# Two products exchanged in their shared bank, weight sums over two attentions, Strassen's form from block 2 on

## The chip, the core and the metric

The kernel runs on one core of a Trainium2 chip. The core has five engines with a queue of instructions each: TensorE (PE; its weight loads are listed as PEld), VectorE (DVE), ScalarE (ACT), GpSimd (POOL) and SyncE (SP), which here mostly issues DMAs. Matmuls write to PSUM, which has 8 banks; one bank holds 128 x 512 values of fp32. The metric is the time of one execution on the device in microseconds (us), as a median over runs.

## The reference

An attention with a relative position bias for 8 batches, 8 heads, 576 positions and head dimension 64, followed by a feed-forward layer with the activation h + sin(alpha h)^2 / alpha:

```python
scores = (q @ k.T) / 8 + bias_table[bucket(|i - j|)]
attn   = exp(scores - max); attn /= attn.sum(-1) + 1e-9
x      = (attn @ v) as [4608 tokens, 512]
h      = x @ w_in                      # 512 -> 2048
g      = h + sin(alpha * h)**2 / (alpha + 1e-9)
out    = g @ w_out                     # 2048 -> 512
```

Inputs and output are fp32 in memory; the kernel multiplies in fp16 and accumulates in fp32.

## The kernel before

There are 8 attentions t = 0 to 7 and 9 blocks of 512 tokens b = 0 to 8. After attention t comes the first half of the feed-forward layer for block t (`plan_moe_in`: for 16 slices f of 128 hidden channels four matmuls into one bank, a sine on ACT, a square on ACT or DVE, and one DVE instruction that writes slice f of the tile g). The second half of block t, g @ w_out, is cut into single matmuls that PE takes as filling work while the attention of t + 1 runs. Block 8 comes after block 7 at the end.

The order of all instructions is worked out when the program is built. `Plan.add` takes a step with its cost on each engine that may do it, what it depends on, a priority and the buffers it needs; `Plan.run` walks through time with these costs, always picks the step that can start first and among those that start together the one with the lowest priority number, and emits it to the queue of the engine that ends it first. So a changed cost can move a step to another engine or change the order of a queue. What waits for what at run time is then set by the dependences of the emitted instructions; between PE and a reader of PSUM they go by bank.

In an attention the scores of a head pair and 128 keys are two matmuls (`qT,kT`; `qT,kt` for the last 64 keys) into a pair of banks among (0,1), (2,3), (4,5); ACT takes the exponential (line 719) into u, or into the tile called nat for the last 64 queries; DVE multiplies a band of it by the exponential of the bias (lines 750, 736, 763, 728); nine matmuls per 128 queries (`vh,u` and eight `v,u`) form the product with v in bank 6 or 7; DVE divides by the row sum (lines 964, 965); and the result reaches xT by a DMA transpose or by PE (line 1036) with a copy on ACT or DVE. Before the first exponential and before the first sine ACT loads a table (line 1403).

The filling work has two forms. A plain row (`plan_mo`) is 128 tokens: 16 matmuls of 512 columns into one bank of tag "mo" (7 or 6), one copy of 128x512 to SBUF by DVE (line 551) and a store. A chain (`plan_chain`) does two such rows by Strassen's form in Winograd's variant: 7 products instead of 8, each of 8 matmuls of 256 columns, where 2k and 2k + 1 share one bank, halves 0 and 1. Products 0 to 5 use banks of tag "mo", product 6 one of tag "st" (any bank). The chain needs four sums of parts of g, each in four pieces of 128x256 on DVE (line 1311), and four sums of quarters of w_out (`wsum`), which are made once in the attention of block 1 (`plan_wsum`, line 1180). DVE reads each product and adds it to what it goes into (`take`, line 1367; the copy of product 0 into the tile zz is on line 551). Blocks 1 to 6 are done as two plain rows and one chain, in the order of MIX = "nnssss"; block 0 as four plain rows; blocks 7 and 8 in another Strassen form (`plan_half`) that the diff leaves alone.

The chain also carries, behind its last product, the step with which POOL copies k and q of attention b + 2 to the staging buffers (`stage_kq`); it depends on the loads of v (`plan_moe_in`) and on the chain's fourth sum. In attention 0 and 1 k and q are turned by PE (`plan_tr`) and copied out of PSUM by DVE or ACT (lines 551 and 549). `plan_late` puts the score units of the last 64 queries of attention 0 at the start of attention 1.

Of the kernel before, what the change touches and what calls it, by code (L numbers as in the profile page):

```python
# [58 lines left out]
class Cell:  # L59
    v = None  # L60
# [178 lines left out]
T_LD = 33.0  # L239

MIX = "nnssss"
CH = ("mo", "mo", "mo", "st")
PIECES = 4
AV_LATE = 9000
# [32 lines left out]
def kernel(  # L277
# [122 lines left out]
    def stage_kq(t):  # L400
        for dst, src in ((staged_k, k), (staged_q, q)):
            nc.gpsimd.dma_start(
                out=dst.ap()[t].rearrange("s (h d) -> s h d", h=H),
                in_=src[t].rearrange("h s d -> s h d"),
            )
# [135 lines left out]
    plan = Plan()  # L541
# [11 lines left out]
    def plan_tr(t, p, kq, pri, nb, deps=()):  # L553

        b, c = Buf("mo"), Cell()

        def mm(e):
            c.v = bank(b).bitcast(F16)
            for i in range(SI):
                x = i * SN  # L560
                if t == 0 and p == 0:
                    nc.tensor.transpose(  # L562
                        out=c.v[:, x : x + SN], in_=natb[:, kq, i], identity=id_sb[0:SN, 0:SN]
                    )
                    continue
                for z in range(2):
                    h = 2 * p - 2 + z if t == 0 else 2 * p + z
                    nc.tensor.transpose(  # L568
                        out=c.v[64 * z : 64 * z + 64, x : x + SN],
                        in_=(nat1 if t == 0 else nat2)[:, kq, h, D * i : D * i + D],  # L570
                        identity=id_sb[0:SN, 0:SN],
                    )

        def cp(e):
            pin = c.v[:, 0:S].rearrange("d (i p) -> d p i", i=SI)

            dst = (kTs, qTs)[kq][t][:, p, :]
            copy_on(e, dst.rearrange("d (p i) -> d p i", i=SI), pin)

        m = plan.add({"PE": 0.4 if t == 0 and p == 0 else 0.5}, mm, deps, pri, nb, new=[b])  # L580
        if t == 0:
            m.pad = (256,) if p else (192,) * (2, 3)[kq]
        eng = {"DVE": 0.75, "ACT": 0.6}
        if t == 0:
            eng = {"ACT": 0.65} if p in T_ACT and kq else {"DVE": 0.75}
        x = plan.add(eng, cp, [m], pri, use=[b])
        if kq:
            return [x], [x]

        def tail(e):  # L590
            for z in range(2):
                r = slice(64 * z, 64 * z + 64)
                k_of(e).tensor_copy(
                    out=kts[t][r, p, r], in_=kTs[t][r, p, 512:S]
                )

        return [x], [plan.add({"POOL": 0.4 if t == 0 else 0.5}, tail, [x], pri + 30)]
# [282 lines left out]
    def plan_late(base, gate):  # L880

        tb, done = tails[0] = Buf("ut"), {}
        units = [(0, "B", 0), (2, "B", 0), (0, "X", 0)]
        made = [plan_unit(0, *x, None, tb, done, gate, base + 30 * k) for k, x in enumerate(units)]

        def run(e):
            for x in made:
                x[2](e)

        m = plan.add({"PE": 0.78}, run, pe_gate, base, new=[tb] + [x[0] for x in made])  # L890
        m.offs = [0.0, 0.1, 0.32, 0.6]
        m.marks = [(x[1], o) for x, o in zip(made, (0.32, 0.54, 0.78))]
        tail_alone(0, base + 1200)
        return [x[3] for x in made]
# [235 lines left out]
    mo_last, kq_in, staged, to_stage = [], [], [], []  # L1130
# [33 lines left out]
    def plan_wsum(t, deps):  # L1164

        n = DM // 2
        quad = [[w_out16[:, NF // 2 * i : NF // 2 * i + NF // 2, n * j : n * j + n] for j in range(2)]
                for i in range(2)]
        todo = (
            (0, quad[0][1], quad[0][0]),  # L1170
            (1, quad[1][1], wsum[:, 0]),
            (2, quad[1][1], quad[0][1]),
            (3, quad[1][0], wsum[:, 1]),
        )
        k, x, y = todo[t]
        for i, d in enumerate(deps):
            r = slice(2 * i, 2 * i + 2)

            def sm(e, k=k, x=x, y=y, r=r):
                nc.vector.tensor_tensor(out=wsum[:, k, r], in0=x[:, r], in1=y[:, r], op=ALU.subtract)  # L1180

            wdone.append(plan.add({"DVE": 0.36}, sm, [d] + wdone[-4:], PB + 9500))

    wdone = []

# [102 lines left out]
    def plan_chain(b, a):  # L1288
# [8 lines left out]
        base = 500000000 + 4 * b + a  # L1297

        def act(i, j):
            return gcell[b].v[:, H2 * j : H2 * j + H2, 128 * (a + i) : 128 * (a + i) + 128]  # L1300
# [17 lines left out]
        def sums(k):  # L1318
            return sv.v[:, 2 * k : 2 * k + 2].rearrange("p k (f t) -> p (k f) t", f=H2 // 2)
# [9 lines left out]
        def prod(k, x, w, deps):  # L1329

            for f in range(H2):

                new = f == 0 and k % 2 == 0

                def mm(e, f=f, new=new):
                    if new:
                        bv[k // 2].v = bank(bk[k // 2])
                    full(at(k), x()[:, f], w()[:, f], f == 0, f == H2 - 1)

                mo_last[:] = [plan.add({"PE": t_pe(n)}, mm, mo_last[:] + deps, base,  # L1340
                                       new=[bk[k // 2]] if new else [],
                                       use=([] if new else [bk[k // 2]]) + [sb, gbuf[b]])]
                mo_last[0].fill = True
                mo_last[0].part = n / DM
            return mo_last[0]
# [4 lines left out]
        def ws(k):  # L1350
            return lambda: wsum[:, k]
# [24 lines left out]
        s2 = pre(lambda: sums(1), lambda: sums(0), lambda: act(0, 0), ALU.subtract, [s1])  # L1376
# [4 lines left out]
        p = prod(1, lambda: act(0, 1), wq(1, 0), [])  # L1381
        c11 = take(1, (0, 0), (2, 0), [p, x], True)
        yield
        p = prod(2, lambda: sums(1), ws(1), [s2, x] + wdone)
        y = take(2, (1, 1), (2, 0), [p, x], True)
        p = prod(3, lambda: act(1, 0), ws(2), [s3])
        v = take(3, (1, 0), (1, 1), [p, y])
        yield
        p = prod(4, lambda: sums(0), ws(0), [])
        w = take(4, (0, 1), (1, 1), [p, y])  # L1390
        c22 = take(4, (1, 1), (1, 0), [p, v, w])
        p = prod(5, lambda: act(1, 1), ws(3), [])
        take(5, (1, 0), (1, 0), [p, v, c22], last=True)
        yield
        p = prod(6, lambda: sums(2), wq(1, 1), [s4])
        take(6, (0, 1), (0, 1), [p, w, c11], last=True)
# [9 lines left out]
    PB = 0  # L1406
# [6 lines left out]
    for t in range(T):  # L1413
        PB = 1000000 * t

        if t > 0:
            gate = [plan.add({"ACT": D_TBL}, lambda e: set_table(EXP_SET), sins, PB)]
        exps = []
        for p in range(NP - 1) if t == 0 else ():
            for kq in range(2):  # L1420
                tr[(0, p + 1, kq)] = plan_tr(0, p + 1, kq, (150, 650, 5)[p], T_PAIR[p][kq])
        if t == 0:
            for g in range(2):
                exps += plan_att0(g, pe_gate, gate)
        else:
            exps += plan_att(t, pe_gate, gate)
            if t == 1:
                for i in range(4):
                    plan_wsum(i, exps[3 * i + 1 : 3 * i + 4] + exps[3 * i + 3 : 3 * i + 4])
            if t == 1:  # L1430
                exps += plan_late(PB + LATE, gate)
        if t == 0:
            for p in range(NP):
                for kq in range(2):
                    tr[(1, p, kq)] = plan_tr(1, p, kq, 10085 + 20 * p, T_TR1[kq])
            plan.add({"POOL": 5.0}, lambda e: stage_kq(2), [], 10090,
                     after=lds + [tr[(1, p, 0)][1][0] for p in range(NP)])

        def swap(e, t=t):
            set_table(SIN_SET)  # L1440
        def turn_in(e, t=t):
            load_kqT(t + 1)
            load_kt(t + 1)

        tbl = [plan.add({"ACT": D_TBL}, swap, exps, PB)]
        if 1 <= t < T - 1:
            kq_in.append(plan.add({"SP": 5.5}, turn_in, [], PB + 9000, after=tbl + [
                x for tt, _, _, x in xdone if tt == t and "SP" in x.engs]))
        if t == T - 1:
            tail_alone(t, PB + 10015)  # L1450
        sins = []
        for b in [t] if t < T - 1 else [t, t + 1]:
            m, s_ = plan_moe_in(b, tbl)
            sins += s_
        pe_gate = [m]
        if t < T - 1:
            if t:
                rows, ch = iter((0, 1)), plan_chain(t, 2)
                for x in MIX:
                    if x == "n":  # L1460
                        plan_mo(t, next(rows))
                    else:
                        next(ch)
            else:
                for a in range(4):
                    plan_mo(t, a)
        else:
            for b in (t, t + 1):
                for a in (0, 2):
                    plan_half(b, a)  # L1470
# [31 lines left out]
```

## Time and profile before

| what | value |
|---|---|
| median of three runs | 369.23 us (368.93 to 372.27) |
| profiled execution | 368.74 us |
| its span in the profile | 366.8 us |
| DMA | 40.53 MB, mean 110 GB/s |
| exponentials, line 719, 128x1024 | 1.03 us each |
| g, line 1094 | 0.74 us each, 144 of them |
| read of a product, line 1367 | 0.42 us each, 30 + 12 of them |

The table's durations are means of groups of instructions in the profiled execution. A record's length isn't the time that an instruction keeps its engine from the next one: neighbours overlap, on PE most of all. Where an engine's throughput matters, starts are compared with starts. The profile also follows the work that ended last backwards from the end (the chain of waits), and lists for each engine in order of time what ran and what ended an idle time before it.

### The profile page before, as it was taken

To read this page: it belongs to the slowest core of one execution; us is meant where nothing else is said; L and a number is where in the kernel's file an instruction comes from. 1 tells how busy PE (TensorE), PEld (TensorE's weight loads), DVE (VectorE), ACT (ScalarE), POOL (GpSimd) and SP (SyncE) were. 2 spreads that over 40 slices of the span, in tenths; PEclk is the share of its full clock that TensorE was granted. 3 is DMA by queue.
4 is the path that set the end of the run, shared out by engine and by line. 5 is a ranking of instruction groups with operands and counts; after the bars stand their busy time and mean duration, and the time that the engine had idled before them with its cause. 6 is when DMAs were issued, how large, how long until landed. Compare 5 with 4: busy or idle time off the path is not lost.

```text
span 366.8 us, 9604 instructions
## 1 busy us (share of the span) xinstructions
PE 356.8 (97%) x3808; PEld 218.9 (60%) x3808; DVE 309.2 (84%) x748; ACT 312.3 (85%) x430; POOL 92.0 (25%) x133
## 2 busy tenths in 40 slices
PE   7889999999999999999999999999999999999996
PEld 3464545644475446885684457545776468456685
DVE  4797979878977998699978998798869997899982
ACT  3988999889897999799988999799979997996711
POOL 7477350064000830047000900082006000000000
PEclk9999999999999999999999999999999999999999
DMA  9999999599724996299917992599529421001122
GB/s 170 198 172 204 200 162 148 115 97 122 111 53 102 127 150 108 78 143 113 152 52 153 87 173 55 134 125 128 104 79 163 35 79 50 15 2 57 44 74 87
DMA packets 150269, 40.53 MB, mean 110 GB/s; under 512 B 137208, under 2 KB 145616, under 8 KB 150224
## 3 DMA queue, kind: packets, MB, share of 16 engines
q0 software_dynamic: 96032, 17.67, 59.6%
q1 hardware_dynamic: 54016, 22.16, 25.9%
q8 instruction: 30, 0.49, 0.6%
q14 instruction: 15, 0.12, 0.1%
q10 hardware_dynamic: 176, 0.09, 0.1%
HBM read 37.73 MB, written 16.56 MB: 148 GB/s over the span
## 4 chain that ended last, share of the span: by engine, by line
PE 83%; ACT 10%; DVE 4%; issue 2%; ACTq 0%
PE pb L469 82%; ACT u L719 8%; ACT s L1080 1%; DVE outs L1367 1%; DVE u L750 1%; ACT sq L1087 1%; PE pb L1036 1%; PE pb L568 0%; ACT kT L549 0%; DVE nat L763 0%; ACT qT L549 0%; DVE xn L965 0%; PE pb L562 0%; DVE qT L551 0%; DVE zz L551 0%
## 5 line engine op out<-in xcount | busy, mean ns | idle before, releaser
L719 ACT ACTIVATE u<-pb 128x1024 f16<-128x1024 f32 (+1 forms) x146 | 136.8, 1022 | 10.3 <-PE pb L469 9.6
L469 PE MATMUL pb<-xT,w_in 128*128 128x512 f16 (+4 forms) x704 | 128.1, 340 | 0.0
L1094 DVE SCALAR_TENSOR_TENSOR g<-sq,inv_a,pb 128x512 f16<-128x512 f16 x144 | 101.1, 743 | 3.7 <-ACT sq L1087 2.0
L1080 ACT ACTIVATE s<-pb,alphaT 128x512 f16<-128x512 f32 x144 | 92.8, 693 | 12.8 <-PE pb L469 12.0
L469 PEld LDWEIGHTS <-w_in 128*128 128x128 f16 x704 | 64.7, 98 | 56.1 <-issue 0.3
L469 PE MATMUL pb<-w_out,g 128*128 128x512 f16 (+1 forms) x416 | 81.7, 339 | 0.5 <-DVE zz L551 0.5
L469 PEld LDWEIGHTS <-g 128*128 128x128 f16 x552 | 51.4, 98 | 37.6 <-issue 7.2
L750 DVE TENSOR_TENSOR u<-u,m2r 128x512 f16<-128x512 f16 (+1 forms) x128 | 61.6, 489 | 11.4 <-ACT u L719 8.6
L469 PEld LDWEIGHTS <-u 128*128 128x128 f16 x1280 | 56.0, 97 | 9.1 <-issue 3.8
L414 POOL COPY kt<-kT 64x256 f16<-64x256 f16 x12 | 5.2, 432 | 172.4 <-DMA kT<-staged_k 142.9
L1087 ACT ACTIVATE sq<-s 128x512 f16<-128x512 f16 x69 | 43.4, 639 | 2.0 <-DVE g L1094 1.1
L469 PE MATMUL pb<-qT,kT 64*128 64x64 f16 (+1 forms) x512 | 42.7, 285 | 1.8 <-DVE qT L551 0.6
L469 PE MATMUL pb<-v,u 128*128 128x65 f16 x1024 | 44.1, 193 | 0.3 <-DVE u L750 0.2
L1089 DVE TENSOR_TENSOR sq<-s 128x512 f16<-128x512 f16 x75 | 31.7, 432 | 10.8 <-ACT s L1080 10.1
L965 DVE TENSOR_TENSOR xn<-pb,rd 128x256 f16<-128x256 f32 (+2 forms) x59 | 28.5, 483 | 2.0
L469 PEld LDWEIGHTS <-kT 64*128 64x128 f16 x512 | 16.1, 94 | 22.4 <-issue 15.4
L469 PE MATMUL pb<-vh,u 128*128 128x130 f16 x128 | 28.2, 221 | 0.1
L419 POOL DMA_DIRECT2D v<-in_v_dram x28 | 24.8, 896 | 3.9 <-DMA nat<-in_k_dram 2.3
L1403 ACT ACT_TABLE_LOAD x15 | 19.2, 1283 | 0.3
L469 PE MATMUL pb<-wsum,g 128*128 128x256 f16 (+1 forms) x136 | 18.6, 266 | 0.9
L719 ACT ACTIVATE nat<-pb 128x1024 f16<-128x1024 f32 (+1 forms) x24 | 17.7, 817 | 0.0
L1367 DVE TENSOR_TENSOR outs<-pb,outs 128x256 f32<-128x256 f32 x30 | 12.6, 421 | 5.3 <-PE pb L469 4.7
(97 smaller groups left out, 303.0 us busy)
## 6 DMA issues: line engine op xcount, KB each, us to landing
out_dram<-outs SPq DMA_DIRECT2D x28, 256.0 KB, 2.9
v<-in_v_dram POOLq DMA_DIRECT2D x28, 128.0 KB, 4.5
staged_k<-in_k_dram POOLq DMA_DIRECT2D x6, 576.0 KB, 8.6
staged_q<-in_q_dram POOLq DMA_DIRECT2D x6, 576.0 KB, 12.4
w_in<-in_moe_w_in_dram POOLq DMA_DIRECT2D x4, 512.0 KB, 8.4
w_out<-in_moe_w_out_dram POOLq DMA_DIRECT2D x4, 512.0 KB, 14.7
out_dram<-outs SPq DMA_DIRECT2D x15, 128.0 KB, 1.7
w_out<-in_v_dram SPq DMA_DIRECT2D x6, 128.0 KB, 4.3
```

The lines of the kernel that those rows point to most:

```text
L414: nc.gpsimd.tensor_copy(out=kts[t % 2][r, :, r], in_=kTs[t % 2][r, :, 512:S])
L419: nc.gpsimd.dma_start(out=vs[t % 2][:, c, :, 0:D], in_=vp[128 * c : 128 * c + 128],)
L469: nc.tensor.matmul(out=out, lhsT=lhsT, rhs=rhs, start=start, stop=stop, skip_group_check=go_on)
L719: nc.scalar.activation(out=o, in_=x, func=AF.Exp, scale=0.125)
L750: nc.vector.tensor_tensor(out=io, in0=io, in1=m2[:, 2 * p : 2 * p + 2, x0 : x0 + hi - lo], op=ALU.mult)
L965: nc.vector.tensor_tensor(out=xn[:, 0:n].rearrange("p c (z d) -> p c z d", z=2), in0=x[:, :, :, 0:D], in1=r.unsqueeze(3).to_broadcast([128 ...
L1080: nc.scalar.activation(out=s16.v, in_=h.v, func=AF.Sin, scale=alphaT[:, f : f + 1])
L1087: nc.scalar.activation(out=sq.v, in_=s16.v, func=AF.Square)
L1089: k_of(e).tensor_tensor(out=sq.v, in0=s16.v, in1=s16.v, op=ALU.mult)
L1094: nc.vector.scalar_tensor_tensor(out=gcell[b].v[:, f, :], in0=sq.v, scalar=inv_a[:, f : f + 1], in1=h.v, op0=ALU.mult, op1=ALU.add,)
L1367: nc.vector.tensor_tensor(out=put(i, j), in0=at(k), in1=put(*x), op=ALU.add)
L1403: nc.scalar.preload_act_table_set(name)
```

## The change

In the chain, the order of products 4 and 5 in their bank is exchanged: the product of act(1,1) with the fourth weight sum is now number 4, that of the first sum of g with the first weight sum number 5. The result of the new product 4 is read last, after the two reads of product 5. Product 2 waited for the weight sums, for a sum of g and for the copy of product 0; the last of these is dropped.

Block 1 is done as four plain rows (FIRST = 2), and its staging step becomes a step of its own without the chain's sum ahead of it. The weight sums are made two in attention 1 and two in attention 2, each in eight pieces of 128x256 instead of four of 128x512, each piece after one exponential of the attention (every second from the third on). Two costs for the planner are lower: an ACT copy in `plan_tr` for attention 1, 0.6 to 0.53, and the late units of attention 0 on PE, 0.78 to 0.5.

```diff
+SUMS = {1: (0, 1), 2: (2, 3)}
+FIRST = 2
...
-        eng = {"DVE": 0.75, "ACT": 0.6}
+        eng = {"DVE": 0.75, "ACT": 0.53}
...
-        m = plan.add({"PE": 0.78}, run, pe_gate, base, new=[tb] + [x[0] for x in made])
+        m = plan.add({"PE": 0.5}, run, pe_gate, base, new=[tb] + [x[0] for x in made])
...
-            r = slice(2 * i, 2 * i + 2)
+            r = slice(i, i + 1)
...
-            wdone.append(plan.add({"DVE": 0.36}, sm, [d] + wdone[-4:], PB + 9500))
+            wdone.append(plan.add({"DVE": 0.218}, sm, [d] + wdone[-8:], PB + 9500))
...
-        p = prod(2, lambda: sums(1), ws(1), [s2, x] + wdone)
+        p = prod(2, lambda: sums(1), ws(1), [s2] + wdone)
...
-        p = prod(4, lambda: sums(0), ws(0), [])
-        w = take(4, (0, 1), (1, 1), [p, y])
-        c22 = take(4, (1, 1), (1, 0), [p, v, w])
-        p = prod(5, lambda: act(1, 1), ws(3), [])
-        take(5, (1, 0), (1, 0), [p, v, c22], last=True)
+        prod(4, lambda: act(1, 1), ws(3), [])
+        p = prod(5, lambda: sums(0), ws(0), [])
+        w = take(5, (0, 1), (1, 1), [p, y])
+        c22 = take(5, (1, 1), (1, 0), [p, v, w])
+        take(4, (1, 0), (1, 0), [p, v, c22], last=True)
...
-            if t == 1:
-                for i in range(4):
-                    plan_wsum(i, exps[3 * i + 1 : 3 * i + 4] + exps[3 * i + 3 : 3 * i + 4])
+            for i in SUMS.get(t, ()):
+                plan_wsum(i, exps[2:18:2])
...
-            if t:
+            if t >= FIRST:
...
             else:
                 for a in range(4):
                     plan_mo(t, a)
+                if to_stage:
+                    n_, x = to_stage.pop()
+                    plan.add({"POOL": 4.5}, lambda e, n_=n_: stage_kq(n_), [x], PB + 9600)
```

## The prediction

> **What bounds the kernel now.** I read the page first, then the chain of waits in order of time, then the timeline of TensorE (PE) beside VectorE (DVE) and ScalarE (ACT) at the places that the diff touches. The page:
>
> ```profile
> span 366.8 us, 9604 instructions
> PE 356.8 (97%) x3808; PEld 218.9 (60%) x3808; DVE 309.2 (84%) x748; ACT 312.3 (85%) x430; POOL 92.0 (25%) x133
> PEclk9999999999999999999999999999999999999999
> PE 83%; ACT 10%; DVE 4%; issue 2%; ACTq 0%
> ```
>
> PE is busy 97% of the span at the full granted clock, and 83% of the chain is PE. Busy alone proves little, because a matmul's record is longer than its turn. So I look at starts: a run of 64 matmuls and a run of 8 half-wide ones.
>
> ```profile
> 112.95 13.98 PE L469 MATMUL pb<-xT,w_in 128*128 128x512 f16 x64
> 145.10 1.04 PE L469 MATMUL pb<-wsum,ss 128*128 128x256 f16 x8
> 100.30 0.27 PE L469 MATMUL pb<-w_out,g 128*128 128x256 f16 x1 [0.51 <-DVE zz L551]
> 309.51 53.78 PE pb L469 x416
> ```
>
> Taking one record (0.38 us for a 512-wide matmul, half of the 0.76 us that two would take end to end; 0.27 us for a 256-wide one, third row) off each run, a 512-wide matmul takes a turn of (13.98 - 0.38) / 63 = 0.216 us and a 256-wide one (1.04 - 0.27) / 7 = 0.11 us, 0.109 over longer runs. Nearly everything on PE goes at those turns, and the last 54 us of the chain are one unbroken PE row. So the kernel is bound by PE's queue: time changes by the turns added or taken, and by the few waits inside that queue. The 2 us of waits on PE that this change can reach are what it is about.
>
> **The wait inside an attention.** First the chain for the attention of block 3, then the timeline of the same place.
>
> ```profile
> 143.88 5.19 PE pb L469 x92
> 149.09 0.42 DVE outs L1367
> 149.52 0.20 DVE nat L763
> 149.72 0.35 DVE outs L1367
> 150.10 1.58 PE pb L469 x13
> ```
>
> ```profile
> 148.78 0.27 PE L469 MATMUL pb<-wsum,g 128*128 128x256 f16 x1
> 148.95 0.41 PE L469 MATMUL pb<-v,u 128*128 128x65 f16 x8
> 149.09 0.42 DVE L1367 TENSOR_TENSOR outs<-pb,outs 128x256 f32<-128x256 f32 x1 [0.39 <-PE pb L469]
> 149.25 0.41 PE L469 MATMUL pb<-v,u 128*128 128x65 f16 x8
> 149.55 0.41 PE L469 MATMUL pb<-v,u 128*128 128x65 f16 x8
> 149.63 0.42 DVE L1367 TENSOR_TENSOR outs<-pb,outs 128x256 f32<-128x256 f32 x1
> 150.10 0.93 PE L469 MATMUL pb<-wsum,g 128*128 128x256 f16 x7
> ```
>
> Product 5 starts (one matmul at 148.78), then attention matmuls run, then its other seven stand until DVE has read product 4 twice out of the same bank, at 149.63 + 0.42 = 150.05. The chain puts 0.42 + 0.20 + 0.35 = 0.97 us of DVE there, but PE was working through the first part of it: one group of v,u begins 0.30 after the other (149.25, 149.55), of which the vh,u matmul between them (130 columns, at the same rate) has 0.06. So the last group's turns ended at 149.55 + 0.24 = 149.79, and PE went on at 150.10. It lost 0.31 us, not 0.97. That distinction carries the forecast.
>
> **The change part by part.**
>
> *Products 4 and 5 exchanged.* The product that is needed only at the end now goes first and is read only after the other is done; both are in the bank before DVE reads anything. In the built program the remaining matmuls of the second product carry no wait on DVE. Five attentions (3 to 7) keep such a chain: 5 x 0.31 = 1.55 us less. The three reads then come back to back after the pair, 2 x 0.35 = 0.7 us later for DVE than before. What hides that is DVE's own idle time behind this place:
>
> ```profile
> 152.49 0.18 DVE L964 RECIPROCAL rd<-pb 128x4 f32<-128x4 f32 x1 [0.80 <-PE pb L469]
> 154.30 0.43 DVE L1089 TENSOR_TENSOR sq<-s 128x512 f16<-128x512 f16 x1 [0.84 <-ACT s L1080]
> ```
>
> 0.80 + 0.84 = 1.64 us of slack against 0.7, and by the pools no other tile asks for that bank before the next block's plain rows. Cost 0; without that cover up to 0.7 each. [...]
>
> *Block 1 without Strassen's form.* Its rows 2 and 3 become 2 x 16 matmuls of 512 columns in place of 7 x 8 of 256: 32 x 0.216 = 6.91 against 56 x 0.109 = 6.10, so +0.81 us of PE turns. [...]
>
> In return the attention of block 2 loses its chain with three waits:
>
> ```profile
> 97.61 2.18 PE L469 MATMUL pb<-w_out,g 128*128 128x512 f16 x14
> 99.83 0.42 DVE L551 COPY zz<-pb 128x256 f32<-128x256 f32 x1 [0.18 <-PE pb L469]
> 102.59 0.60 PE L469 MATMUL pb<-w_out,g 128*128 128x256 f16 x4
> 103.30 0.22 PE L469 MATMUL pb<-vh,u 128*128 128x130 f16 x1
> 110.22 0.41 PE L469 MATMUL pb<-v,u 128*128 128x65 f16 x8
> 110.77 0.92 PE L469 MATMUL pb<-wsum,g 128*128 128x256 f16 x7
> ```
>
> The group of 14 (3 of 512 columns, 11 of 256; the row names the first form) ends at 97.61 + 2.18 = 99.79 by its records; its last matmul began 0.27 earlier and had its turn until 0.11 after that, 99.63. The next came at 100.30: 0.67 lost (the 0.51 in brackets, in the row further up, counts from the record's end). Four at 102.59 end their turns at 103.03; the next came at 103.30: 0.27. And 110.22 + 0.24 = 110.46 against 110.77: 0.31. Sum 1.25 us less. DVE is relieved there too, which is worth nothing by itself. What is late next in a plain attention is PE behind the exponentials: three score groups in flight, freed by ACT. The attention of block 1 is plain already, and shows what that costs:
>
> ```profile
> 49.32 1.00 PE L469 MATMUL pb<-qT,kT 64*128 64x512 f16 x6
> 59.69 0.82 PE L469 MATMUL pb<-qT,kT 64*128 64x512 f16 x6
> ```
>
> Six score matmuls undisturbed take 0.82; once they took 1.00. So 0.2 us of new waits in attention 2, between 0 and 0.4.
>
> *The first chain moves to the attention of block 3,* whose products are now laid out as in the row at 99.83: in the built program product 1 starts four matmuls (0.44 us) ahead of a wait for the copy of product 0. The copy costs, from the row, 0.18 of delay, 0.42 of work and 0.05 back to PE, 0.65 in all: 0.2 us lost if DVE is free, 0.7 if it stands behind another eviction, 0 if the planner's order hides it as in the attentions behind. I take 0.25.
>
> *Weight sums.* In place of 16 subtractions of 512 columns in attention 1 there are 16 of 256 columns in it and 16 in attention 2.
>
> ```profile
> L1180 DVE TENSOR_TENSOR wsum<-w_out 128x512 f16<-128x512 f16 x8 | 3.3, 419 | 0.0
> L1311 DVE TENSOR_TENSOR ss<-g 128x256 f16<-128x256 f16 x24 | 5.7, 284 | 0.0
> ```
>
> DVE goes from 16 x 0.42 = 6.7 us to 32 x 0.284 = 9.1, 4.5 in each attention. [...] Attention 1 has 2.2 us less DVE work than before and attention 2 trades 16 pre-sums of 0.284 for 16 of these, so no engine that bounds is touched: 0. The first user is now the chain in attention 3, a block later than the last sum.
>
> *Planner costs.* The lower ACT cost (0.6 to 0.53) moves one copy of qT from DVE to ACT, ahead of the table load of attention 1; the lower PE cost of the late units lets PE put one plain matmul more ahead of the next scores.
>
> ```profile
> 42.15 0.75 ACT L549 ACTIVATE kT<-pb 128x576 f16<-128x576 f16 x1
> 42.68 1.37 ACT L1080 ACTIVATE s<-pb,alphaT 128x512 f16<-128x512 f32 x2
> 45.72 0.65 ACT L549 ACTIVATE kT<-pb 128x576 f16<-128x576 f16 x1
> 46.39 1.28 ACT L1403 ACT_TABLE_LOAD   x1
> 47.69 2.21 ACT L719 ACTIVATE nat<-pb 128x1024 f16<-128x1024 f32 x3
> 72.52 0.49 ACT L549 ACTIVATE xT<-pb 128x384 f16<-128x384 f16 x1 [1.27 <-PE pb L1036]
> ```
>
> Such a copy takes a turn of 42.68 - 42.15 = 0.53 us on ACT, and ACT's only long idle time after it is the 1.27 us that end at 72.52, behind the exponentials. PE waits for exponentials at 49.32 already, so up to 0.53 goes on PE, less the one matmul of 0.22 put ahead: I take 0.3 (0 to 0.53).
>
> *Staging of block 3's k and q* is planned without the chain's sum in front. On POOL's queue the built order is the same instruction for instruction, and on SP's two stores change places with transposes: 0.
>
> Sum: -1.55 - 1.25 + 0.81 + 0.2 + 0.25 + 0.3 = -1.24 us. The profiled execution took 368.74 us (span 366.8 and 1.94 around it), which gives 367.5; the median of the three runs is 369.23, 0.5 above, which gives 368.0. I say 367.8.
>
> **The rivals.**
>
> *The waits move and nothing is left* (0.16). ACT is 85% busy and in attentions almost gapless; if the exponentials rather than PE's turns set the pace, the 0.31 waits reappear at the score matmuls. For it: the ACT rows in the chain (10%). Against: before the first s of a block and at the next exponentials ACT waits for PE, as the 1.27 us row shows for one, so what PE gains ACT gains. Only the 1.25 - 0.81 of block 1 would remain, less 0.75 for the new waits: 368.74 + 0.3 = 369.0, 369.5 by the median.
>
> *Slower: DVE cannot take three reads in a row* (0.08). The place is the end of attentions 3 to 7; it decides once DVE's 1.64 us of slack is used up, so that the first g of a block, and with it the banks that the next score or w_in matmuls need, come late. Price 2 x 0.35 = 0.7 each: 5 x 0.7 - 1.55 - 1.25 + 0.81 + 0.75 = +2.26, 371.0; with all three exposed (1.05) +4.0, 372.7, both from the profiled execution. Against it: the two idle rows above.
>
> *The chain is right: all of DVE's 0.97 goes* (0.04). Six attentions x 0.97, 0.95 more for the two other waits of attention 2, less 0.81 and 0.75: -5.2, 363.5. Against it: PE's starts.
>
> *The exchange does not take the wait away* (0.04), because another read of that bank falls between the two products: the five 0.31 stay, 369.0. Against it: no wait stands in the built order.
>
> *Plain rows are the cheaper form* (0.01). If 512-wide matmuls ran denser than the row of 64 shows, by up to 0.81 us in all, the +0.81 goes: 366.7. Against it: that row. [...]
>
> **How the numbers follow.** The forecast has 0.67. Its own range: with the three unknown costs at zero -2.0 (366.7), with all at their upper ends (0.4, 0.7, 0.53) -0.4 (368.4), and 0.5 up for the median at the upper end: 366.7 to 368.9. To hold 8 in 10 I take in the first and fourth rival and the 0.3 us by which the lower two runs differ: 366.3 to 369.8. About 1% (3.7 us) is what a measurement of this kernel can tell from no change. Faster by over 1% would need the third rival, 0.04, and a little for waits that I missed: 0.05. Slower by over 1% is the upper end of the second, with something for an unseen stall: 0.05. Within 1%: 0.90.
>
> **What would show it.** In the profile after: no DVE row in the chain between the attention's matmuls and the second product of the pair, in attentions 3 to 7, and block periods 0.3 us shorter; attention 2 without a wait for zz, its w_out matmuls all 512 wide; a wait of PE for zz in attention 3; the table load of attention 1 some 0.5 us later against the copies ahead of it, with PE's next score matmuls stretched by about 0.3. I would be wrong if DVE had no idle left at the block's first s, or if PE had idle rows for ACT that it does not have now.

## The result, and the profile after

Eight runs of the changed kernel have a median of 367.03 us (366.63 to 368.27), eight of the kernel before 369.38 (368.69 to 372.27). The ratio is 0.9935 with a 95% interval of 0.9911 to 0.996 (it is estimated over the runs, as all ratios below are, and differs a little from that of the medians): the change saves 0.4 to 0.9%. The profiled executions took 367.10 and 368.74, 1.64 us apart.

The page of the changed kernel: span, busy times, and the shares of the chain of waits by engine.

```profile
span 365.2 us, 9550 instructions
PE 356.7 (98%) x3784; PEld 216.2 (59%) x3784; DVE 304.5 (83%) x737; ACT 314.5 (86%) x435; POOL 91.7 (25%) x133
PE 84%; ACT 7%; DMA 5%; POOL 2%; DVE 1%; issue 0%
```

DVE has gone from 4% of the chain to 1%. The chain over attention 3 and the start of attention 4 shows what that 1% is (start, us, what):

```profile
135.89 5.88 PE pb L471 x60
141.77 0.02 issue
141.79 0.44 DVE zz L553
142.23 0.04 issue
142.27 8.84 PE pb L471 x156
```

Before, two reads of a product and a DVE step between them stood in this chain at 149.09 to 150.07. Now PE runs through that place, and DVE appears once, with the copy of product 0. The timeline of PE and DVE at the exchanged pair of attention 3:

```profile
147.86 1.04 PE L471 MATMUL pb<-wsum,g 128*128 128x256 f16 x8
149.39 0.41 PE L471 MATMUL pb<-v,u 128*128 128x65 f16 x8
149.64 1.04 PE L471 MATMUL pb<-wsum,ss 128*128 128x256 f16 x8
```

```profile
150.74 0.88 DVE L1369 TENSOR_TENSOR outs<-pb,outs 128x256 f32<-128x256 f32 x2
151.91 0.18 DVE L966 RECIPROCAL rd<-pb 128x4 f32<-128x4 f32 x1 [0.29 <-PE pb L471]
152.47 0.41 DVE L1369 TENSOR_TENSOR outs<-pb,outs 128x256 f32<-128x256 f32 x1
153.72 0.42 DVE L1091 TENSOR_TENSOR sq<-s 128x512 f16<-128x512 f16 x1 [0.84 <-ACT s L1082]
```

The second product (149.64) starts 0.25 us after the last group of v,u, which is that group's turn: nothing is lost. DVE makes the two reads of product 5 together, and the one of product 4 behind a division. Its idle time ahead of the division has shrunk from 0.80 to 0.29 us; the 0.84 before the first square are untouched.

PE's starts give the time by stage. The table has the start of the first score matmul of each attention, and of the last matmul, minus that of the kernel before (us, each from the timeline of one profiled execution):

| start of | changed | exchange alone | all but the exchange | first chain in block 1 | narrow sums early |
|---|---|---|---|---|---|
| attention 1 | -0.22 | -0.36 | -0.27 | -0.12 | -0.09 |
| attention 2 | -0.43 | -0.35 | -0.54 | +1.36 | +1.51 |
| attention 3 | -0.66 | -0.44 | -0.76 | +1.64 | +1.40 |
| attention 4 | -0.57 | -0.97 | -0.23 | +1.34 | +1.49 |
| attention 5 | -0.65 | -1.27 | -0.22 | +1.03 | +1.18 |
| attention 6 | -0.96 | -1.57 | -0.22 | +0.73 | +0.88 |
| attention 7 | -1.26 | -1.88 | -0.22 | +0.43 | +0.58 |
| last matmul | -1.56 | -2.18 | -0.22 | +0.12 | +0.27 |

From one row to the next, an attention with an exchanged pair is 0.30 us shorter wherever nothing else happens in it. The first row is spread of the start-up; the last section says what it goes with.

### The profile page after: what moved, and what is told of

Read it like the earlier page. It is cut to its first block, busy times and chain, and to the rows that moved or that the text cites. A ratio compares the mean times of both kernels' runs of the same rounds, so it can differ in the third digit from the quotient of the medians.

```text
span 365.2 us, 9550 instructions
## 1 busy us (share of the span) xinstructions
PE 356.7 (98%) x3784; PEld 216.2 (59%) x3784; DVE 304.5 (83%) x737; ACT 314.5 (86%) x435; POOL 91.7 (25%) x133
## 4 chain that ended last, share of the span: by engine, by line
PE 84%; ACT 7%; DMA 5%; POOL 2%; DVE 1%; issue 0%
PE pb L471 83%; ACT u L721 7%; DMA w_out<-in_moe_w_out_dram 5%; POOL w_out L457 0%; PE pb L1038 0%; DVE u L752 0%; POOL nat L446 0%; PE pb L564 0%; DVE qT L553 0%; PE pb L570 0%; DVE zz L553 0%; DVE xn L967 0%; POOL u L738 0%; POOL vh L465 0%; POOL vh L464 0%
## 5 line engine op out<-in xcount | busy, mean ns | idle before, releaser
L471 PE MATMUL pb<-w_out,g 128*128 128x512 f16 (+1 forms) x432 | 88.3, 344 | 0.7 <-DVE zz L553 0.5
L1089 ACT ACTIVATE sq<-s 128x512 f16<-128x512 f16 x71 | 44.6, 640 | 1.9 <-DVE g L1096 1.1
L1091 DVE TENSOR_TENSOR sq<-s 128x512 f16<-128x512 f16 x73 | 30.4, 424 | 9.4 <-ACT s L1082 8.7
L551 ACT ACTIVATE u<-pb 128x256 f32<-128x256 f32 x12 | 4.6, 386 | 14.7 <-PE pb L471 14.7
L404 POOL DMA_DIRECT2D staged_q<-in_q_dram x6 | 16.4, 2740 | 0.0
```

The source lines that it names most:

```text
L404: nc.gpsimd.dma_start(out=dst.ap()[t].rearrange("s (h d) -> s h d", h=H), in_=src[t].rearrange("h s d -> s h d"),)
L471: nc.tensor.matmul(out=out, lhsT=lhsT, rhs=rhs, start=start, stop=stop, skip_group_check=go_on)
L1089: nc.scalar.activation(out=sq.v, in_=s16.v, func=AF.Square)
L1091: k_of(e).tensor_tensor(out=sq.v, in0=s16.v, in1=s16.v, op=ALU.mult)
```

## The experiments

**Which part brings the time.** Two kernels split the change: the kernel before with only products 4 and 5 exchanged, and the changed kernel with only that taken back.

```diff
 # exchange alone; the other kernel has the inverse edit
-        p = prod(4, lambda: sums(0), ws(0), [])
-        w = take(4, (0, 1), (1, 1), [p, y])
-        c22 = take(4, (1, 1), (1, 0), [p, v, w])
-        p = prod(5, lambda: act(1, 1), ws(3), [])
-        take(5, (1, 0), (1, 0), [p, v, c22], last=True)
+        prod(4, lambda: act(1, 1), ws(3), [])
+        p = prod(5, lambda: sums(0), ws(0), [])
+        w = take(5, (0, 1), (1, 1), [p, y])
+        c22 = take(5, (1, 1), (1, 0), [p, v, w])
+        take(4, (1, 0), (1, 0), [p, v, c22], last=True)
```

> The kernel before with nothing but products 4 and 5 exchanged, in all six chains. Theory (PE's queue): the second product's 0.31 us wait goes six times, 1.9 us in all, ratio to the kernel before 0.995, and PE's starts show the second product right behind the attention's matmuls. Rival (the chain of waits counts): 6 x 0.97 = 5.8 us less, ratio 0.984. Rival (three reads in a row are too much for DVE): no gain or a loss, ratio 1.000 or more.

> The changed kernel with products 4 and 5 in the old order. Theory: five waits of 0.31 us come back, 1.5 us over the changed kernel's 367.0, so about 368.6 and a ratio of 0.998. If the exchange were not what counts: 367.0, ratio 0.9935.

The exchange alone: 366.95 us (366.46 to 371.02, 12 runs; before 368.71), ratio 0.9961 (0.9932 to 0.999). Everything but the exchange: 368.94 (368.32 to 372.38, 12 runs), ratio 1.0023 (0.9996 to 1.005). In the profiles the first saves 1.82 us between the start of attention 1 and the last matmul, the second costs 0.05. The exchange alone shortens attention 2 by only 0.09 and attention 3 by 0.53, because one matmul of 512 columns (0.22) is done in attention 2 instead of 3; with that set right both are 0.31 as well. So the exchange is the change as far as time goes. The rest gives back what it takes: where the exchange alone keeps its chain in block 1, its attention 2 still has the wait for the copy of product 0,

```profile
97.25 2.18 PE L469 MATMUL pb<-w_out,g 128*128 128x512 f16 x14
99.95 0.27 PE L469 MATMUL pb<-w_out,g 128*128 128x256 f16 x1 [0.52 <-DVE zz L551]
```

and in the changed kernel the same wait stands in attention 3:

```profile
140.83 0.93 PE L471 MATMUL pb<-w_out,g 128*128 128x256 f16 x7
142.27 0.27 PE L471 MATMUL pb<-w_out,g 128*128 128x256 f16 x1 [0.52 <-DVE zz L553]
```

By starts both are 0.68 us: seven turns of 0.109 from 140.83 end at 141.59, and the next matmul comes at 142.27. Of the changed kernel's row of seven, three matmuls belong to product 0 and four to product 1. DVE's copy of product 0:

```profile
141.79 0.42 DVE L553 COPY zz<-pb 128x256 f32<-128x256 f32 x1 [0.31 <-PE pb L471]
```

Product 0 has its last start at 140.83 + 2 x 0.109 = 141.05, and DVE is free from 141.48, but the copy begins when all seven have ended (140.83 + 0.93 = 141.76). It waits for the four matmuls of product 1 too, which are in the same bank and stand ahead of it in the built order. Their number does not matter: three stood there before the change, and five stand there in the last kernel below, and by starts the wait is 0.68 us each time.

**The planner's two costs.** The changed kernel with 0.6 and 0.78 put back.

```diff
-        eng = {"DVE": 0.75, "ACT": 0.53}
+        eng = {"DVE": 0.75, "ACT": 0.6}
-        m = plan.add({"PE": 0.5}, run, pe_gate, base,
+        m = plan.add({"PE": 0.78}, run, pe_gate, base,
```

> The changed kernel with the two planner costs of before (0.6 and 0.78). Only the place of one qT copy and of one plain matmul differ. The prediction's step: 0.3 us faster than the changed kernel (366.7). The profile after, where the first w_in matmul behind this attention keeps the 0.22 us that it had gained at the start: no difference (367.0 within 0.2), because ACT's delay is taken out of idle time that it has later in the same attention.

Measured 367.14 us (366.50 to 370.77, 6 runs), ratio 0.9947 (0.9929 to 0.9966): level with the changed kernel. The profiles say more than the medians can. ACT in the changed kernel at attention 1:

```profile
45.50 0.65 ACT L551 ACTIVATE kT<-pb 128x576 f16<-128x576 f16 x1
46.03 0.66 ACT L551 ACTIVATE qT<-pb 128x576 f16<-128x576 f16 x1
46.71 1.28 ACT L1405 ACT_TABLE_LOAD   x1
```

The copy of qT has joined ACT, and the table load comes 1.24 us after the attention's first score matmul instead of 0.71. In the same place PE of the changed kernel waits for the load of w_out:

```profile
46.20 2.75 PE L471 MATMUL pb<-w_out,g 128*128 128x512 f16 x12
49.15 0.59 PE L471 MATMUL pb<-w_out,g 128*128 128x512 f16 x2 [0.20 <-DMA w_out<-in_moe_w_out_dram]
```

That transfer is also the 5% of DMA in the chain; by starts the wait is 0.36 us. With the old costs attention 1 with its block is 0.29 us shorter (43.42 against 43.71) at the same number of matmuls. That execution waits for the same transfer, though no idle time is printed there: by starts 0.29 us, with the load landing at 52.93 and the matmul starting at 52.98. With this wait taken off, the stage lasts 43.13 us with the old costs, and 43.34 or 43.35 in the five profiles that share the changed kernel's attention 1 (the changed kernel, the one without the exchange, and three of those below), although their waits for w_out range from 0.31 to 0.71. So the two costs are worth 0.22 us here, by one profile of the old ones, which the spread of the medians hides.

**Are plain rows as dear as their starts say?** The changed kernel with no chain in any block of 2 to 6.

```diff
-FIRST = 2
+FIRST = 9
```

> The changed kernel with plain rows in blocks 1 to 6, no chain left. Theory: five times 0.81 us of PE turns more, 4.05, less what the chains still wait (0.68 for zz in the attention of block 3, 0.27 at a score matmul in each of the four behind): +2.3 to +4.0 over the changed kernel, 369.3 to 371.0. Rival (512-wide matmuls run denser than the profile's 0.216 us): 367 or less. DVE's load falls by some 5 us per attention, which theory prices at nothing.

Measured 369.88 us (369.19 to 374.72, 12 runs), 2.85 above the changed kernel; ratio 1.0032 (1.0004 to 1.006). Five blocks at +0.81 would be 4.05; the plain rows have no wait for the copy of product 0 (0.68, once) and no 0.27 us wait at the scores (four times). From the start of attention 1 to the last matmul the profiles differ by 2.29 us, which is 4.05 less these, so a chain is worth about 0.46 us a block net there, 0.57 by the medians. A matmul of 512 columns is not cheaper than its 0.216 us.

**Has DVE room for the three reads?** The changed kernel with two more additions of 128x256 out of the same bank behind the last read, into the scratch tile zz, in each of the five chains.

```diff
+                if k == 4:
+                    for _ in range(2):
+                        nc.vector.tensor_tensor(out=put(2, 0), in0=at(k), in1=put(*x), op=ALU.add)
```

> The changed kernel with two more DVE additions of 128x256 (results thrown away, into the scratch tile zz) right behind the last read of the pair, in each of the five chains; the planner does not know of them. Theory: DVE has some 0.9 us of idle time left behind this place, the two take 0.7, so the time stays within 0.2 us of 367.0. Rival (the reads are on the path): 5 x 0.7 = 3.5 us more, 370.5.

Measured 367.09 us (366.59 to 368.22, 12 runs), ratio 0.9938 (0.991 to 0.9966): no change. DVE at the end of attention 3 in this kernel:

```profile
153.19 0.41 DVE L1369 TENSOR_TENSOR outs<-pb,outs 128x256 f32<-128x256 f32 x1
153.64 0.88 DVE L1372 TENSOR_TENSOR zz<-pb,outs 128x256 f32<-128x256 f32 x2
154.45 0.43 DVE L1091 TENSOR_TENSOR sq<-s 128x512 f16<-128x512 f16 x1
```

The 0.84 us ahead of the first square are now filled to the end, and the square starts right behind; by these rows one more read would have made it late, which was not run. The rival "DVE cannot take three reads" fails, and the margin was just two reads.

**The first chain back in block 1.** With the gain of the exchange in hand, keeping block 1 in Strassen's form should save 0.8 us of turns.

```diff
-SUMS = {1: (0, 1), 2: (2, 3)}
-FIRST = 2
+SUMS = {1: (0, 1, 2, 3)}
+FIRST = 1
```

> The changed kernel with Strassen's form from block 1 on again and all weight sums (still 32 pieces of 128x256) in the attention of block 1. Theory: 0.81 us of PE turns less, the 0.68 us wait for zz in the attention of block 3 gone (and the 0.27 at a score matmul back); in the attention of block 2 the built order has no lone matmul waiting for zz, so its old waits of 0.67 and 0.27 come back in part or not at all. Between 367.1 (all of them back) and 366.0 (none): faster than the changed kernel or equal. If plain rows in block 1 are what the change gained by: 367.5 or more.

Measured 369.03 us (368.46 to 372.64, 12 runs), ratio 1.0014 (0.9976 to 1.0051): a miss by two microseconds. The table shows nearly all of the loss in one place, ahead of attention 2. All 32 narrow subtractions are now due in attention 1, and 20 of them (4 in the changed kernel) come only after its last matmul with v, 14 of these among the squares and g of block 1. DVE, and then ACT up to the table load of attention 2, in this kernel:

```profile
84.64 0.28 DVE L1182 TENSOR_TENSOR wsum<-w_out,wsum 128x256 f16<-128x256 f16 x1
84.84 0.42 DVE L1091 TENSOR_TENSOR sq<-s 128x512 f16<-128x512 f16 x1
85.18 0.28 DVE L1182 TENSOR_TENSOR wsum<-w_out,wsum 128x256 f16<-128x256 f16 x1
```

```profile
88.42 1.24 ACT L1089 ACTIVATE sq<-s 128x512 f16<-128x512 f16 x2
89.46 0.78 ACT L1082 ACTIVATE s<-pb,alphaT 128x512 f16<-128x512 f32 x1
90.27 0.63 ACT L1089 ACTIVATE sq<-s 128x512 f16<-128x512 f16 x1
90.92 1.28 ACT L1405 ACT_TABLE_LOAD   x1
```

In the changed kernel the same table load is at

```profile
88.60 1.28 ACT L1405 ACT_TABLE_LOAD   x1
```

The subtractions push squares from DVE to ACT (ACT does 13 of the 16 of block 1 instead of 8), and the exponentials of attention 2 begin 2.3 us later. Two runs tell the sums from the chain: narrow sums early without the chain, and the chain with the wide sums of the kernel before (16 of 512 columns).

```diff
 # narrow sums early
-SUMS = {1: (0, 1), 2: (2, 3)}
+SUMS = {1: (0, 1, 2, 3)}
```

```diff
 # chain in block 1, wide sums
-FIRST = 2
+FIRST = 1
-            r = slice(i, i + 1)
+            r = slice(2 * i, 2 * i + 2)
-            wdone.append(plan.add({"DVE": 0.218}, sm, [d] + wdone[-8:], PB + 9500))
+            wdone.append(plan.add({"DVE": 0.36}, sm, [d] + wdone[-4:], PB + 9500))
...
-            for i in SUMS.get(t, ()):
-                plan_wsum(i, exps[2:18:2])
+            if t == 1:
+                for i in range(4):
+                    plan_wsum(i, exps[3 * i + 1 : 3 * i + 4] + exps[3 * i + 3 : 3 * i + 4])
```

> The changed kernel with all 32 narrow subtractions of the weight sums in attention 1, and block 1 still in plain rows. Theory (the weight sums cost the time: those that do not fit into attention 1 fall between the g of block 1 on DVE, squares move to ACT, the next table load comes late): attention 2 begins some 1.5 us later than in the changed kernel, as in the kernel with the chain in block 1, and the median is 368.3 to 368.9. Rival (the chain in block 1 cost the time): 366.8 to 367.3, attention 2 no later than in the changed kernel.

> The changed kernel with its first chain in block 1 and the weight sums as 16 subtractions of 512 columns in attention 1, as before the change. Theory (weight sums): no loss before attention 2, 366.7 to 367.3, level with the changed kernel and with the exchange alone. Rival (the chain in block 1): 368.8 to 369.3, as with narrow sums.

Narrow sums early: 368.82 us (368.28 to 372.10, 12 runs), ratio 1.0004 (0.9977 to 1.0031), with the same late start of attention 2, although PE fills part of the gap with five plain matmuls (1.08 us) that the changed kernel does later. Chain in block 1 with wide sums: 367.67 (366.82 to 371.12, 12 runs), ratio 0.9963 (0.9932 to 0.9995), its span 364.9, and attention 2 at -0.14. The median lies above its expectation by 0.4, the lowest run within it. The loss is the sums', not the chain's. But this does not show that DVE lacks room for 32 of them in attention 1. In the source each narrow piece waits for the eight ahead of it, and the eighth of a sum for the 17th exponential of the attention. So only the first eight are spread over the attention (53.90 to 69.87 us with narrow sums early), and the other 24 can only follow them at its end. Wide pieces are released by exponentials 2 to 13, and all 16 are done before the attention's last matmul with v. Whether 32 narrow pieces released as early would fit was not run; in the order that they have, they need the second attention that the change gives them.

The last of this group has wide sums in attention 1 and block 1 plain (the edit above without FIRST = 1).

> The changed kernel with the weight sums as 16 subtractions of 512 columns in attention 1 and block 1 in plain rows. If the narrow form and the split over two attentions are worth nothing in time once block 1 is plain: 366.8 to 367.3. If the relief of DVE in attention 1 hid the prediction's 0.3 us for the copy moved to ACT: attention 2 begins 0.3 us later than in the changed kernel, 367.3 to 367.6.

367.31 us (367.09 to 367.62, 6 runs), ratio 0.9954 (0.9936 to 0.9972): between the two expectations. Attention 1 and its block took 1.1 us longer than in the changed kernel, but with the three plain matmuls (0.65) that the changed kernel leaves for later, and with a longer wait for the load of w_out:

```profile
49.50 0.59 PE L471 MATMUL pb<-w_out,g 128*128 128x512 f16 x2 [0.65 <-DMA w_out<-in_moe_w_out_dram]
```

So narrow and split against wide and early is worth 0.3 us by the medians and 0.56 by these profiles from attention 1 on, of which 0.45 is the longer wait for that transfer; what is left is too small to tell.

**Can the copy of product 0 be treated in the same way?** Product 1 first, then the read of product 0, in all chains; and the same with the first chain in block 1.

```diff
-        x = take(0, (2, 0), None, [p])
         p = prod(1, lambda: act(0, 1), wq(1, 0), [])
+        x = take(0, (2, 0), None, [p])
```

> The changed kernel with product 0 read only after product 1, the same idea as the exchange for the first pair. Theory: the 0.68 us wait for zz in the attention of block 3 goes and nothing else changes: 366.4. If something else is queued behind it: 367.0.

> Both together: chains from block 1 on, weight sums in one attention, product 0 read after product 1. Theory: 0.81 less of PE turns and no wait for zz anywhere: 1.2 us under the changed kernel, 365.8, the best of all. If the wait only moves to product 2 (whose bank needs the eviction): 366.5 to 367.

368.63 us (368.08 to 369.08, 12 runs), ratio 0.9973 (0.9944 to 1.0003), and 369.76 (368.76 to 373.41, 12 runs), ratio 1.0009 (0.9975 to 1.0043): both missed. The wait for zz is gone from attention 3, and two others stand there:

```profile
143.87 0.27 PE L471 MATMUL pb<-w_out,g 128*128 128x256 f16 x1
144.91 0.60 PE L471 MATMUL pb<-wsum,ss 128*128 128x256 f16 x4 [0.77 <-DVE xn L967]
147.57 1.58 PE L471 MATMUL pb<-wsum,g 128*128 128x256 f16 x13 [0.35 <-DVE outs L1369]
```

By starts they are 0.93 and 0.51 us, in place of 0.68. The first is a wait for the division that frees product 2's bank, the second one of product 3 for the read of product 2, in whose bank it is. The edit also did more than change an order: the planner now gives the copy of product 0 to ACT in all five chains, where the changed kernel has it on DVE in all five. There it stands among the exponentials. In attention 5, ACT and then PE:

```profile
221.10 0.40 ACT L551 ACTIVATE zz<-pb 128x256 f32<-128x256 f32 x1
222.47 0.39 PE L471 MATMUL pb<-qT,kT 64*128 64x512 f16 x2 [0.38 <-ACT u L721]
```

By starts that score matmul waits 0.54 us, where the changed kernel's waits 0.26, and attentions 5 to 7 are 0.28 us longer each. The later reading itself, with the copy left on DVE, was not run. What sets products 4 and 5 apart is that nothing in the chain but the end of one output waits for product 4, while the reads of products 1 to 3 take zz, or what was made from it, as their other operand. The second kernel also has the narrow sums in one attention, and with them the loss of the kernel with the first chain in block 1.

**A different place for the first chain.** On top of the chain in block 1 with wide sums, its first products ahead of the plain rows, in that attention alone.

```diff
-                for x in MIX:
+                for x in ('ssnnss' if t == 1 else MIX):
```

> As the kernel with wide sums and the chain in block 1, but in attention 2 alone the chain's first two pairs of products come ahead of the two plain rows. In its built order five matmuls of product 1 instead of three precede the wait for the copy of product 0, and that wait no longer comes with scores behind it in a plain stretch: the 0.68 and 0.28 us of attention 2 shrink by some 0.5 us, 366.3 to 366.7. Rival (the waits move to the later products or to the scores, as they did where product 0 was read late): 367.0 to 368.6.

372.91 us (372.21 to 373.60, 6 runs), ratio 1.0105 (1.0083 to 1.0126): the worst of all, and the rival's range was too narrow as well. PE at attention 2:

```profile
88.61 1.03 PE L471 MATMUL pb<-qT,kT 64*128 64x512 f16 x4 [1.53 <-DVE g L1096]
90.00 0.39 PE L471 MATMUL pb<-qT,kT 64*128 64x512 f16 x2 [0.36 <-DVE g L1096]
93.76 0.49 PE L471 MATMUL pb<-w_out,g 128*128 128x256 f16 x3 [0.52 <-DVE zz L553]
99.89 0.60 PE L471 MATMUL pb<-wsum,g 128*128 128x256 f16 x4 [0.56 <-DVE outs L1369]
```

The wait for zz is 0.68 us by starts, as before, and PE, with no plain row to do, now also stands at the attention's start behind the last g. Against the kernel before, this one loses 5.4 us between the start of attention 2 and the w_in of block 3. Nearly half of that is work moved, not waits: attention 1 with its block has 64 plain matmuls instead of 77, and with the missing ones to do PE has 2.5 us more of turns in that stretch. The rest beyond these rows was not followed.

## Why the prediction was right

The time of 367.8 was 0.8 above the measured 367.03, in the range, and the forecast's mechanism is the one found. The sum of -1.24 us became -1.34 in the profiles from attention 1 on. That it came so near owes something to luck: behind the exchanges the errors of three terms, -0.43, +0.17 and +0.14, nearly cancel. Step by step:

- *The wait is 0.31 us, not the chain's 0.97.* Shown: attentions 5, 6 and 7 are 0.31, 0.30 and 0.30 us shorter, and the exchange alone gains the same in each of its six. The rival of 0.97 each is out.
- *Five exchanges, -1.55.* Right: the difference between the kernel with and without the exchange is 1.39 us from attention 1 to the last matmul in the profiles, 1.9 by medians. In attention 4 the changed kernel shows 0.08 shorter because it does one more plain matmul there, 33 instead of 32, which is 0.22.
- *DVE's cover of 0.7 us.* Right, and tested: two reads more cost nothing (367.09 us against 367.03). The third read did not follow the others directly but stood behind a division.
- *Block 1 plain against attention 2's three waits.* Predicted +0.81 - 1.25 + 0.2 = -0.24 us. Attention 2 with its block is 0.23 shorter, while PE does 1.24 us more turns there, 0.65 of them left over from attention 1 and its block. So 1.47 us of waits went, 0.43 more than the forecast's 1.05 net. The new score waits did not come, PE of the changed kernel having no idle row in attention 2. And the prediction overlooked a wait of 0.16 within its group of 14: product 0 began at 98.43, 0.38 after the last matmul of 512 columns and right behind the division that freed its bank (DVE, 97.82 to 98.38).
- *The first chain's wait in attention 3.* This term was mis-sized: 0.25 predicted, 0.68 measured. The prediction let the 0.44 us of product 1's four matmuls cover the copy's 0.65. They cover nothing, since the copy waits for them as well: the wait begins when they end, whatever their number. The prediction's own rows showed it, with the copy at 99.83, 0.04 after the end of the group of 14, and the wait of 0.67 that it counted there was the price to take. A wait of 0.26 at a score matmul of the same attention (143.88 before) went, which the prediction did not see, so the term is +0.42 net against 0.25.
- *Planner costs, +0.3.* The mechanism is shown (the table load 0.53 us later against the attention's start), and its price is 0.22 by one profile with the old costs; the medians show no difference. Attention 1 with its block became 0.21 shorter with three plain matmuls (0.65) fewer, so 0.44 us was lost, of which 0.36 is the wait for w_out. In the kernel before that load had landed (48.83) before PE came to it (49.01). The prediction did not look at that transfer at all, so that 0.44 lies near 0.3 is luck.
- *Weight sums and staging, 0.* Nothing in the profiles speaks against it as changed, though the staging step was not run alone. But the claim was made of DVE's sum of work, and the runs show that the place decides: the same 32 subtractions, released in one attention, cost 1.8 us by medians (368.82 against 367.03).

The rival "plain rows are the cheaper form" fails: the all-plain kernel is 2.85 us slower by the medians, and a run of 64 matmuls of 512 columns still takes 0.216 us a matmul in the changed kernel. The rest of the change, which the prediction put at +0.31 without its exchanges, is +0.21 in the changed kernel's profile with five times 0.31 set aside, and +0.05 in the kernel without the exchange.

The result of 2.35 us between medians is 0.7 more than between the profiled runs; the kernel before had medians from 368.71 to 369.38 in the four sets of runs, so the spread is wide enough for that 0.7; a gain that the profiles hide is not shown.

## What to carry to other kernels

Where two products share a PSUM bank, put the one that nothing else needs first and read the bank only when both are written; in these runs a reader between them waited for the matmuls already queued to that bank, and the next ones waited for the reader: 0.31 us at products 4 and 5, 0.68 at product 0. Then look in the built order at what else moved: the same edit on the first pair, whose first result feeds the later reads, also sent a copy to ScalarE, 86% busy in the changed kernel, and did not pay (368.63 us against 367.03). Price a wait on TensorE by start against start with the turn taken off: here that gave 0.31 where the chain of waits gave 0.97 and came out within 0.01. Work on an engine with slack was free only where the slack was: two more reads (0.88 us) in VectorE's idle time cost nothing, and 16 subtractions of 0.28 us that their dependences held back into the stage behind an attention shifted other work to ScalarE and cost 1.8 us.

## What the runs showed of the hardware

The profiled execution with the old planner costs took 370.77 us while the other five runs of that kernel took 366.5 to 367.4. Its matmuls at the start are longer. First that execution, then the changed kernel:

```profile
10.28 0.61 PE L471 MATMUL pb<-qT,kT 64*128 64x512 f16 x2
19.40 1.46 PE L471 MATMUL pb<-qT,kT 64*128 64x512 f16 x6
21.45 0.28 PE L471 MATMUL pb<-zz 128*128 128x256 f16 x1
```

```profile
9.06 0.39 PE L471 MATMUL pb<-qT,kT 64*128 64x512 f16 x2
19.31 0.39 PE L471 MATMUL pb<-qT,kT 64*128 64x512 f16 x2
```

Two score matmuls take 0.61 instead of 0.39, and attention 1 begins at 49.36 instead of 45.47. The trace's records of the granted clock go with this. The first of them, at full clock, begins at 20.93 us in that execution, at 5.76 in the changed kernel's and between 3.92 and 6.68 in the other twelve profiles; it is where the short matmuls begin: in that execution a matmul of 256 columns on zz takes 0.39 at 19.07, 0.33 at 20.79 and 0.28 at 21.45. The profile's pages show full clock from the start, because they print time without such a record as 1.00. Both executions begin with ten matmuls of 512 columns in 3.91 us, from 1.27 in that one and from 1.26 in the changed kernel's; the matmuls behind them stayed long for almost 16 us in the one and for 0.6 in the other. What sets the moment, the traces do not show.

The 0.1 to 0.7 us by which attention 1 starts apart in the other profiles are not of this kind: the one with the latest full clock among them (6.68) begins attention 1 at 44.99, the kernel before (4.65) at 45.68. They go with the time at which DVE first multiplies by the tile mhr in attention 0, which ranges from 16.88 to 17.81 us. In two profiles DVE stands there for the load of mhr. The earliest, the kernel with the chain ahead of the plain rows (attention 1 at 44.99), and the latest, the all-plain kernel (45.99):

```profile
16.88 0.21 DVE L738 TENSOR_TENSOR u<-u,mhr 128x128 f16<-128x128 f16 x1
```

```profile
17.81 0.23 DVE L738 TENSOR_TENSOR u<-u,mhr 128x128 f16<-128x128 f16 x1 [0.23 <-DMA mhr<-e_dram]
```

That the load sets the spread was not tested. The stages above are compared from the start of attention 1 on because of it.
